# Merging the weight loads and pairing two K tiles at the start of a decode kernel, with V moved to the low regions of the buffer

## The chip, the cores and the metric

One core of a Trainium2 chip (trn2). The metric is the device time of one execution in microseconds (us). The runs of the kernel before lie within about 0.1% of each other. A profile is one execution; its span is shorter than the timed execution (before: 381.4 against 383.2). A run would be set aside as slow if it took over 1.5% more than the fastest of the same kernel. The engines' names: PE multiplies matrices, PEld loads its weights, DVE is the vector engine, ACT (ScalarE) the scalar one, POOL is GpSimd, and SP here only issues loads.

## The reference, cut to what matters

One decode step. Attention with 32 query heads over 4 K/V heads of 65,536 positions by 128 (here: S = 65536, four heads of K and V, 134 MB in bfloat16), and beside it a gated MLP on the same row x. Sizes of the weights: wq 1024x4096, w_in 1024x3584, w_out 1792x1024, wo 4096x1024.

```python
q = (x @ wq)                                  # 32 heads of 128
scores = einsum('bhqd,bhkd->bhqk', q, k) * Dh ** -0.5
a = einsum('bhqk,bhkd->bhqd', softmax(scores), v) ... @ wo
z = gelu(x @ w_in); z1, z2 = halves of z      # z2 goes through a layernorm
b = (z1 * (w_sp * layernorm(z2) + b_sp)) @ w_out
g = sigmoid((x * gate_w).sum())
return g * a + (1 - g) * b
```

Everything is read once: 162.01 MB.

## The kernel before

All large inputs go through one SBUF buffer `kv` of five regions (0 to 4), 32 KB in each of 128 partitions. A K or V tile of one head (one of four) fills one region. All large loads are issued by one engine's queue (SP), in program order, and each waits until the instructions that last used its region are done. The 16 DMA engines then take the loads in that order.

```python
NKV = 5                                        # regions
def load(src, shape, at): ...                  # one DMA into region `at`
def load_kv(src, g, j, at, n=1): ...           # n tiles of head g from tile j on, one DMA

win_t = [load(win_view[:, i * KH:(i + 1) * KH, :], (KH, F), 3 + i) for i in range(2)]
wq_t = [load(wq_view[:, i * KH:(i + 1) * KH, :], (KH, HD), 1 - i) for i in range(2)]
...
def k_tile(g, j, kn):                          # scores of one K tile
    for v in range(VC):                        # four quarters
        nc.vector.transpose(...)               # DVE, 2.3 us
        while late:
            nc.vector.reduce_max(**late.pop()) # row maximum of the tile before
        ...                                    # 8 matmuls
    nc.scalar.copy(out=sct[g, j][:], in_=s_ps[:])
def stats(g): ...                              # maximum, exponentials, transposes of p
def v_tile(g, j, vt): ...                      # 32 matmuls
...
build_w(0)
for j in range(NT):                            # head 0
    k_tile(0, j, load_kv(A_k_cache, 0, j, (2, 1, 0, 3)[j])[0])
    if j == 1:
        build_w(1)
project(load(B_w_out..., (FC, D), 4), FC, uT, 0, first=True)
stats(0)
for g in range(1, G):
    for h in range(2):
        kn = load_kv(A_k_cache, g, 2 * h, 1 - h, 2)
        for i in ((0, 1), (1, 0))[h]:
            k_tile(g, 2 * h + i, kn[i])
        if h == 0 and g + 1 < G:
            build_w(g + 1)
        vn = load_kv(A_v_cache, g - 1, 2 * h, 3, 2)
        v_tile(g - 1, 2 * h, vn[0])
        if h == 1:
            stats(g)
        v_tile(g - 1, 2 * h + 1, vn[1])
    head_out(g - 1)
for j, n, at in ((0, 2, 1), (2, 1, 3), (3, 1, 4)):
    ...                                        # last V tiles, then wo in pieces, then the output
```

In what follows K1.23 means tiles 2 and 3 of K's head 1, loaded as one pair.

Of the kernel before, what the change touches and what calls it, by code (L numbers as in the profile page):

```python
# [22 lines left out]
ZN = 448  # L23
HN = 512
WO_SPLIT = ((16,), (8, 4, 2, 1, 1))
# [3 lines left out]
def kernel(  # L29
# [17 lines left out]
    _, _, D = A_x.shape  # L47
    _, G, S, DH = A_k_cache.shape
    HD = A_wq.shape[1]
    H = HD // DH  # L50
    REP = H // G
    F = B_w_in.shape[1]
    FH = F // 2
    KC = D // P
    FC = FH // P
    OC = HD // P
    QD = P // H
    NT = S // (P * CT)
# [20 lines left out]
    def same_weights(ins):  # L79
        held.add(ins.ins.name)  # L80
# [79 lines left out]
    def load(src, shape, at):  # L160
        n = 1
        for s in shape:
            n *= s
        v = kv[:, int(at * CT * P):int(at * CT * P) + n]
        if len(shape) == 2:
            v = v.rearrange("p (a b) -> p a b", b=shape[1])
        ins = nc.sync.dma_start(out=v, in_=src)  # L167
        if not first_load:
            first_load.append(ins.ins.name)
        return v  # L170

    def load_kv(src, g, j, at, n=1):
        h, i = divmod(j, 2)
        rows = src[0, g, 2 * h * CT * P:2 * (h + 1) * CT * P, :].rearrange(
            "(p c) d -> p (c d)", c=2 * CT)
        v = load(rows[:, i * CT * DH:(i + n) * CT * DH], (n * CT * DH,), at)
        return [v[:, i * CT * DH:(i + 1) * CT * DH] for i in range(n)]
# [8 lines left out]

    KH = KC // 2
    win_view = B_w_in.rearrange("(p c) n -> p c n", c=KC)
    win_t = [load(win_view[:, i * KH:(i + 1) * KH, :], (KH, F), 3 + i) for i in range(2)]
    wq_view = A_wq.rearrange("(p c) n -> p c n", c=KC)  # L190
    wq_t = [load(wq_view[:, i * KH:(i + 1) * KH, :], (KH, HD), 1 - i) for i in range(2)]


    row = const.tile([P, P], FP32, name="row")
# [25 lines left out]
    def one_hot(shape, dtype, in0, col, name):  # L220
# [13 lines left out]
                     start=True, stop=True)  # L234
# [37 lines left out]
    def x_rows(ps, w, n, i):  # L272
        for c in range(KH):
            for t in range(NB):
                for k in range(F // (NB * ZN) if n == ZN else NHB):
                    o = (k * NB + t) * n
                    ins = nc.tensor.matmul(  # L277
                        ps[t * B:(t + 1) * B, k * HN:k * HN + n],
                        lhsT=xT[:, i * KH + c:i * KH + c + 1].to_broadcast([P, B]),
                        rhs=w[:, c, o:o + n], start=(i == 0 and c == 0),  # L280
                        stop=(i == 1 and c == KH - 1), skip_group_check=True)
                    if k > 0:
                        same_weights(ins)

    z_ps = pss.tile([P, 2 * HN], FP32, name="z_ps", tag="s")
    for i in range(2):
        x_rows(z_ps, win_t[i], ZN, i)
    rowt = big.tile([P, 2 * HN], FP32, name="rowt")
    om8 = rowt[:].rearrange("p (x d) -> p x d", d=DH)
    zm = rowt[:, :2 * ZN].rearrange("p (h j c) -> p h j c", h=2, c=FC)  # L290
# [41 lines left out]
    uT = const.tile([P, FC], BF16, name="uT")  # L332
# [3 lines left out]

    q_ps = pss.tile([P, 2 * HN], FP32, name="q_ps", tag="s")
    for i in range(2):
        x_rows(q_ps, wq_t[i], HN, i)
    NX = NHB * HH * 2  # L340
    qm = rowt[:].rearrange("p (x j e) -> p x j e", x=NX, e=2)
    for k in range(NHB):
# [3 lines left out]
                                                                   j=B, e=2),  # L346
# [11 lines left out]
                     rhs=q4[:].rearrange("p t x -> p (t x)"), start=True, stop=True)  # L358
# [8 lines left out]
    def build_w(g):  # L367
        for v in range(VC):
            nc.vector.tensor_tensor(
                out=wt[g % 2][:, v, :, :, v, :],  # L370
                in0=qs[:, g].unsqueeze(2).to_broadcast([P, BP, NB, REP]),
                in1=own_n[:].unsqueeze(1).unsqueeze(3).to_broadcast([P, BP, NB, REP]),
                op=ALU.mult)
# [5 lines left out]
    def k_tile(g, j, kn):  # L379
        kb = kn.bitcast(I32)  # L380
        n = CC * DH // 2
        s_ps = pss.tile([P, 2 * HN], FP32, name="s_ps", tag="s")
        for v in range(VC):
            nc.vector.transpose(out=kb[:, v * n:(v + 1) * n], in_=kb[:, v * n:(v + 1) * n])  # L384
            while late:
                nc.vector.reduce_max(**late.pop())  # L386
            kx = kn[:, v * CC * DH:(v + 1) * CC * DH].rearrange(
                "p (c h k e) -> p h e c k", h=2, k=B, e=2)
            for b in range(BP):
                for k in range(2):  # L390
                    ins = nc.tensor.matmul(  # L391
                        s_ps[:, k * HN:(k + 1) * HN],
                        lhsT=wt[g % 2][:, v, b].rearrange("p a v h -> p (a v h)"),
                        rhs=kx[:, b // 2, b % 2, k * CC // 2:(k + 1) * CC // 2, :],
                        start=(v == 0 and b == 0), stop=(v == VC - 1 and b == BP - 1),
                        skip_group_check=True)
                    if k > 0:
                        same_weights(ins)
        if g not in mxs:
            mxs[g] = wk.tile([P, NT], FP32, name="mx")  # L400
        sct[g, j] = scp.tile([P, CC * B], BF16, name="sc")
        nc.scalar.copy(out=sct[g, j][:], in_=s_ps[:])  # L402
        late.append(dict(out=mxs[g][:, j:j + 1], in_=sct[g, j][:], axis=AX.X))
# [26 lines left out]
    def v_tile(g, j, vt):  # L430
        if j == 0:
            o_ps[g] = pso.tile([P, 2, VC * DH], FP32, name="o_ps")
        vx = vt.rearrange("p (v c d) -> p c v d", v=VC, d=DH)
        for u in range(CC // 2):
            hs = slice(u % 2 * P // 2, (u % 2 + 1) * P // 2)
            for e in range(2):
                ins = nc.tensor.matmul(  # L437
                    o_ps[g][hs, e, :],
                    lhsT=ptt[g, j][:, 2 * u:2 * u + 2, :].rearrange("p c x -> p (c x)"),
                    rhs=vx[:, 2 * u + e], start=(j == 0 and u < 2),  # L440
                    stop=(j == NT - 1 and u >= CC // 2 - 2), skip_group_check=True)
                if e > 0:
                    same_weights(ins)
# [31 lines left out]
    def project(w, n, vec, c0, first=False, last=False):  # L475
        for c in range(n):
            for t in range(NB):
                nc.tensor.matmul(  # L478
                    out_ps[t * B:(t + 1) * B, :],
                    lhsT=vec[:, c0 + c:c0 + c + 1].to_broadcast([P, B]),  # L480
                    rhs=w[:, c, t * NO:(t + 1) * NO],
                    start=(first and c == 0), stop=(last and c == n - 1),
                    skip_group_check=True)


    build_w(0)
    for j in range(NT):
        k_tile(0, j, load_kv(A_k_cache, 0, j, (2, 1, 0, 3)[j])[0])
        if j == 1:
            build_w(1)  # L490
    project(load(B_w_out.rearrange("(p c) n -> p c n", c=FC), (FC, D), 4), FC, uT, 0, first=True)
    stats(0)
    for g in range(1, G):
        for h in range(2):
            kn = load_kv(A_k_cache, g, 2 * h, 1 - h, 2)
            for i in ((0, 1), (1, 0))[h]:
                k_tile(g, 2 * h + i, kn[i])
            if h == 0 and g + 1 < G:
                build_w(g + 1)
            vn = load_kv(A_v_cache, g - 1, 2 * h, 3, 2)  # L500
            v_tile(g - 1, 2 * h, vn[0])
            if h == 1:
                stats(g)
            v_tile(g - 1, 2 * h + 1, vn[1])
        head_out(g - 1)
    for j, n, at in ((0, 2, 1), (2, 1, 3), (3, 1, 4)):
        for i, vt in enumerate(load_kv(A_v_cache, G - 1, j, at, n)):
            v_tile(G - 1, j + i, vt)
    head_out(G - 1)
# [1 line left out]

    wo_view = A_wo.rearrange("(p c) n -> p c n", c=OC)
    c0 = 0
    for at, split in enumerate(WO_SPLIT):
        for n in split:
            t = load(wo_view[:, c0:c0 + n, :], (n, D), at + c0 % (OC // 2) * D / (CT * P))
            project(t, n, oa, c0, last=(c0 + n == OC))
            c0 += n
# [46 lines left out]
```

## Time and profile before

| kernel before | |
|---|---|
| time | 383.24 us (median of 3), 383.21 (5, later) |
| span of the profile | 381.4 us |
| DMA, read from HBM | 162.01 MB, 425 GB/s over the span |
| busy: PE / DVE / ACT | 61% / 57% / 10% |

The page of the kernel before: busy tenths of the DMA engines in 40 slices of the span, what they moved in each, and the sum.

```profile
DMA  9999999999999999999999999999999999999995
GB/s 376 439 426 416 433 436 440 436 461 429 400 426 440 440 435 426 440 440 440 440 428 440 440 440 433 428 427 406 433 440 428 426 433 427 440 411 436 440 405 230
HBM read 162.01 MB, written 0.00 MB: 425 GB/s over the span
```

The DMA row is full up to the last slice. Throughput in three stretches (start:end, length, busy time of PE, PEld, DVE, ACT and POOL, PE's clock, mean busy share of the DMA engines, GB/s):

```profile
core 0: us, PE busy (x) PEld busy (x) DVE busy (x) ACT busy (x) POOL busy (x), PEclk, DMA share, GB/s
40.00:90.00 50.00, 32.56 (x140) 6.28 (x65) 42.28 (x35) 3.04 (x3) 0.00 (x0) 0.84 1.00 430
90.00:170.00 80.00, 50.23 (x273) 11.67 (x167) 47.97 (x33) 10.29 (x14) 0.00 (x0) 0.80 1.00 433
170.00:370.00 200.00, 130.26 (x727) 30.22 (x373) 114.94 (x96) 22.71 (x33) 0.00 (x0) 0.83 1.00 431
```

430 to 433 GB/s throughout. The Trainium skill ("DMA: Bandwidth & Descriptors", Specifications) gives 435 GB/s as the ceiling of the fabric, and the trace agrees. So the kernel is bound by DMA, and what matters is whether the DMA queue ever runs empty. That is read from when SP issues a load. The timeline of SP (start us, duration, what):

```profile
71.85 0.33 SPq L167 DMA_DIRECT2D kv<-in_A_k_cache_dram  x1
95.97 0.33 SPq L167 DMA_DIRECT2D kv<-in_A_v_cache_dram  x1
119.21 0.33 SPq L167 DMA_DIRECT2D kv<-in_A_k_cache_dram  x1
137.86 0.33 SPq L167 DMA_DIRECT2D kv<-in_A_v_cache_dram  x1
```

These four are K1.01, V0.01, K1.23 and V0.23. The packet records of the trace say when the engines came to them: the mean of the 16 engines had finished the load ahead of V0.01 at 105.3, of K1.23 at 124.7 and of V0.23 at 144.1 us. So each was issued 5.5 to 9 us before it was needed. Call that the lead: the mean time at which the engines finish all that was issued earlier, less the time of the issue.

DVE after head 0's first K tile (the number in brackets is idle time, and what ended it):

```profile
59.84 2.31 DVE L384 STREAM_TRANSPOSE kv<-kv 128x2048 int32<-128x2048 int32 x1 [2.12 <-DMA kv<-in_A_k_cache_dram]
62.07 1.20 DVE L386 TENSOR_REDUCE mx<-sc 128x1 f32<-128x1024 bf16 x1
63.18 6.69 DVE L384 STREAM_TRANSPOSE kv<-kv 128x2048 int32<-128x2048 int32 x3
```

DVE waits 2.1 us for tile 1, which lands while PE still works on tile 0.

### The profile page before, as it was taken

What the parts mean: (1) busy time and instruction counts of PE and PEld (TensorE: products, weight loads), DVE (VectorE), ACT (ScalarE), POOL (GpSimd) and SP (SyncE); (2) the same over time, 40 slices, a digit from 0 to 9 for tenths busy, and PEclk for the clock granted to TensorE, in tenths of its full rate; (3) what the DMA queues carried; (4) which work ended last, traced back from release to release, by engine and by line L of the source; (5) the groups of instructions that cost most, each with busy time, mean ns of one, the idle gap of its engine ahead of it and who ended that gap; (6) DMA issues with size and microseconds to landing.
All of it is one profiled execution on the core that took longest, in us unless ns stands there. A gap on an engine that the chain in (4) does not pass through costs nothing.

```text
span 381.4 us, 2581 instructions
## 1 busy us (share of the span) xinstructions
PE 232.4 (61%) x1372; PEld 56.8 (15%) x796; DVE 218.4 (57%) x211; ACT 39.6 (10%) x55; POOL 4.4 (1%) x10
## 2 busy tenths in 40 slices
PE   0433467678157944796397629872967196849355
PEld 0110011112011210121011101120111011212123
DVE  4241487996687506966977059669780488550040
ACT  1010001111601100114010001050001010500000
POOL 4000000000000000000000000000000000000000
PEclk9966659998759895989588959895799679969766
DMA  9999999999999999999999999999999999999995
GB/s 376 439 426 416 433 436 440 436 461 429 400 426 440 440 435 426 440 440 440 440 428 440 440 440 433 428 427 406 433 440 428 426 433 427 440 411 436 440 405 230
DMA packets 4375, 162.17 MB, mean 425 GB/s; under 512 B 520, under 2 KB 524, under 8 KB 908
## 3 DMA queue, kind: packets, MB, share of 16 engines
q1 hardware_dynamic: 4324, 162.01, 98.7%
q8 instruction: 8, 0.13, 0.1%
q14 instruction: 3, 0.02, 0.0%
q10 hardware_dynamic: 40, 0.01, 0.0%
HBM read 162.01 MB, written 0.00 MB: 425 GB/s over the span
## 4 chain that ended last, share of the span: by engine, by line
DMA 59%; PE 20%; DVE 16%; issue 2%; ACT 1%; SPq 1%; DVEq 0%; ACTq 0%
DMA kv<-in_A_k_cache_dram 37%; PE s_ps L391 15%; DVE kv L384 9%; DMA kv<-in_A_wo_dram 8%; DMA kv<-in_A_wq_dram 7%; DMA kv<-in_A_v_cache_dram 7%; PE o_ps L437 3%; DVE pt L427 2%; DVE mx L386 1%; DVE o_sb L451 1%; PE q_ps L277 1%; ACT sc L424 1%; DVE rowt L447 1%; ACT sc L402 1%; SPq L167 1%
## 5 line engine op out<-in xcount | busy, mean ns | idle before, releaser
L391 PE MATMUL s_ps<-kv,wt 128*128 128x512 bf16 x512 | 142.1, 437 | 81.8 <-DVE kv L384 81.7
L384 DVE STREAM_TRANSPOSE kv<-kv 128x2048 int32<-128x2048 int32 x64 | 142.7, 2280 | 55.5 <-DMA kv<-in_A_k_cache_dram 55.5
L437 PE MATMUL o_ps<-kv,pt 128*64 128x512 bf16 x512 | 61.6, 399 | 7.7 <-DMA kv<-in_A_v_cache_dram 7.7
L391 PEld LDWEIGHTS <-wt 128*128 128x128 bf16 x256 | 27.5, 108 | 197.6 <-issue 140.2
L402 ACT CAST sc<-s_ps 128x1024 bf16<-128x1024 f32 x16 | 16.2, 1013 | 253.5 <-PE s_ps L391 253.5
L437 PEld LDWEIGHTS <-pt 128*64 128x64 bf16 x256 | 16.0, 115 | 50.7 <-issue 48.1
L427 DVE STREAM_TRANSPOSE pt<-sc 128x1024 bf16<-128x1024 bf16 x16 | 18.6, 1217 | 6.8 <-ACT sc L424 6.8
L386 DVE TENSOR_REDUCE mx<-sc 128x1 f32<-128x1024 bf16 x12 | 14.5, 1207 | 10.1 <-ACT sc L402 10.1
L424 ACT ACTIVATE sc<-sc,nb 128x1024 bf16<-128x1024 bf16 x16 | 18.2, 1137 | 12.2 <-DVE nb L420 12.2
L447 DVE TENSOR_TENSOR rowt<-o_ps,own 128x1024 f32<-128x1024 f32 x4 | 4.8, 1194 | 24.9 <-PE o_ps L437 24.9
L457 PE MATMUL om_ps<-o_sb,hsel 128*32 128x128 f32 x8 | 2.5, 421 | 19.7 <-DVE o_sb L451 19.7
L406 DVE TENSOR_REDUCE mx<-sc 128x1 f32<-128x1024 bf16 x4 | 4.9, 1220 | 14.2 <-ACT sc L402 14.2
L277 PE MATMUL q_ps<-kv,xT 128*32 128x512 bf16 x64 | 7.2, 627 | 7.4 <-DMA kv<-in_A_wq_dram 7.4
L478 PE MATMUL out_ps<-kv,oa 128*32 128x256 bf16 x128 | 6.7, 366 | 3.7 <-DMA kv<-in_A_wo_dram 2.2
L277 PE MATMUL z_ps<-kv,xT 128*32 128x448 bf16 x64 | 6.2, 570 | 3.8 <-DMA kv<-in_B_w_in_dram 3.8
L344 DVE TENSOR_TENSOR rowt<-q_ps,own_b 128x512 f32<-128x512 f32 x2 | 1.3, 686 | 12.5 <-PE q_ps L277 12.5
L451 DVE TENSOR_REDUCE o_sb<-rowt 128x128 f32<-128x1024 f32 x4 | 7.5, 1872 | 0.1
L292 DVE TENSOR_TENSOR rowt<-z_ps,own_b 128x448 f32<-128x448 f32 x2 | 1.2, 620 | 8.5 <-PE z_ps L277 8.5
L233 PE MATMUL xb_ps<-xg,spread 8*128 8x256 bf16 x1 | 0.4, 367 | 9.1 <-DMA xg<-in_gate_w_dram 9.1
L277 PEld LDWEIGHTS <-xT 128*32 128x32 bf16 x64 | 3.0, 139 | 19.4 <-issue 19.3
L478 PEld LDWEIGHTS <-oa 128*32 128x32 bf16 x128 | 4.4, 124 | 6.1 <-issue 3.3
L521 ACT CAST out_sb<-out_ps 128x256 bf16<-128x256 f32 x1 | 0.4, 372 | 45.4 <-PE out_ps L478 45.4
(88 smaller groups left out, 54.8 us busy)
## 6 DMA issues: line engine op xcount, KB each, us to landing
kv<-in_A_k_cache_dram SPq DMA_DIRECT2D x4, 4096.0 KB, 26.8
kv<-in_A_wq_dram SPq DMA_DIRECT2D x2, 4096.0 KB, 32.8
kv<-in_A_v_cache_dram SPq DMA_DIRECT2D x2, 4096.0 KB
kv<-in_B_w_in_dram SPq DMA_DIRECT2D x2, 3584.0 KB, 15.0
kv<-in_A_wo_dram SPq DMA_DIRECT2D x1, 4096.0 KB
kv<-in_B_w_out_dram SPq DMA_DIRECT2D x1, 3584.0 KB
kv<-in_A_wo_dram SPq DMA_DIRECT2D x1, 2048.0 KB, 28.6
kv<-in_A_wo_dram SPq DMA_DIRECT2D x1, 1024.0 KB, 30.7
```

Of the source, the lines that this page charges most:

```text
L277: ins = nc.tensor.matmul(ps[t * B:(t + 1) * B, k * HN:k * HN + n], lhsT=xT[:, i * KH + c:i * KH + c + 1].to_broadcast([P, B]), rhs=w[:, c, ...
L384: nc.vector.transpose(out=kb[:, v * n:(v + 1) * n], in_=kb[:, v * n:(v + 1) * n])
L386: nc.vector.reduce_max(**late.pop())
L391: ins = nc.tensor.matmul(s_ps[:, k * HN:(k + 1) * HN], lhsT=wt[g % 2][:, v, b].rearrange("p a v h -> p (a v h)"), rhs=kx[:, b // 2, b % 2, ...
L402: nc.scalar.copy(out=sct[g, j][:], in_=s_ps[:])
L406: nc.vector.reduce_max(**late.pop())
L424: nc.scalar.activation(out=sct[g, j][:], in_=sct[g, j][:], func=ACT.Exp, scale=SCALE, bias=nb[:, 0:1], accum_out=lss[g][:, j:j + 1])
L427: nc.vector.transpose(out=ptt[g, j][:].rearrange("p c x -> p (c x)"), in_=sct[g, j][:])
L437: ins = nc.tensor.matmul(o_ps[g][hs, e, :], lhsT=ptt[g, j][:, 2 * u:2 * u + 2, :].rearrange("p c x -> p (c x)"), rhs=vx[:, 2 * u + e], sta ...
L447: nc.vector.tensor_tensor(out=om8, in0=o_ps[g][:].rearrange("p e (v d) -> p (e v) d", d=DH), in1=own_8[:].unsqueeze(2).to_broadcast([P, 2 ...
L451: nc.vector.tensor_reduce(out=o_sb[:], in_=om8.rearrange("p x d -> p d x"), axis=AX.X, op=ALU.add)
L478: nc.tensor.matmul(out_ps[t * B:(t + 1) * B, :], lhsT=vec[:, c0 + c:c0 + c + 1].to_broadcast([P, B]), rhs=w[:, c, t * NO:(t + 1) * NO], st ...
```

## The change

Its intent is fewer and larger loads: w_in as one load of 56 KB a partition and wq as one of 64 KB (each was two halves); in head 0, K tiles 0 and 1 as a pair behind tile 2, so that the stream is tile 2, pair 0 and 1, tile 3. To make room, the regions are mirrored: V goes to regions 0 and 1, K's pairs to 2 to 4.

```diff
-    win_t = [load(win_view[:, i * KH:(i + 1) * KH, :], (KH, F), 3 + i) for i in range(2)]
+    win_t = load(win_view, (KC, F), 3)
-    wq_t = [load(wq_view[:, i * KH:(i + 1) * KH, :], (KH, HD), 1 - i) for i in range(2)]
+    wq_t = load(wq_view, (KC, HD), 0)
 ... (the matmuls on them take w[:, i * KH + c, ...]) ...
-    for j in range(NT):
-        k_tile(0, j, load_kv(A_k_cache, 0, j, (2, 1, 0, 3)[j])[0])
-        if j == 1:
+    for j, n, at in ((2, 1, 2), (0, 2, 3), (3, 1, 1)):
+        for i, kn in enumerate(load_kv(A_k_cache, 0, j, at, n)):
+            k_tile(0, j + i, kn)
+        if j == 2:
             build_w(1)
-    project(load(B_w_out..., (FC, D), 4), FC, uT, 0, first=True)
+    project(load(B_w_out..., (FC, D), 0), FC, uT, 0, first=True)
     stats(0)
     for g in range(1, G):
         for h in range(2):
-            kn = load_kv(A_k_cache, g, 2 * h, 1 - h, 2)
-            for i in ((0, 1), (1, 0))[h]:
+            kn = load_kv(A_k_cache, g, 2 * h, 2 + h, 2)
+            for i in ((1, 0), (0, 1))[h]:
 ...
-            vn = load_kv(A_v_cache, g - 1, 2 * h, 3, 2)
+            vn = load_kv(A_v_cache, g - 1, 2 * h, 0, 2)
 ... (the last V tiles and wo are mirrored alike) ...
```

More of the change, by code (lines that the diff above doesn't have):

```diff
@@ L279, in x_rows @@
                         lhsT=xT[:, i * KH + c:i * KH + c + 1].to_broadcast([P, B]),
-                        rhs=w[:, c, o:o + n], start=(i == 0 and c == 0),
+                        rhs=w[:, i * KH + c, o:o + n], start=(i == 0 and c == 0),
                         stop=(i == 1 and c == KH - 1), skip_group_check=True)
@@ L286 @@
     for i in range(2):
-        x_rows(z_ps, win_t[i], ZN, i)
+        x_rows(z_ps, win_t, ZN, i)
     rowt = big.tile([P, 2 * HN], FP32, name="rowt")
@@ L338 @@
     for i in range(2):
-        x_rows(q_ps, wq_t[i], HN, i)
+        x_rows(q_ps, wq_t, HN, i)
     NX = NHB * HH * 2
@@ L486 @@
     build_w(0)
-    for j in range(NT):
-        k_tile(0, j, load_kv(A_k_cache, 0, j, (2, 1, 0, 3)[j])[0])
-        if j == 1:
+    for j, n, at in ((2, 1, 2), (0, 2, 3), (3, 1, 1)):
+        for i, kn in enumerate(load_kv(A_k_cache, 0, j, at, n)):
+            k_tile(0, j + i, kn)
+        if j == 2:
             build_w(1)
-    project(load(B_w_out.rearrange("(p c) n -> p c n", c=FC), (FC, D), 4), FC, uT, 0, first=True)
+    project(load(B_w_out.rearrange("(p c) n -> p c n", c=FC), (FC, D), 0), FC, uT, 0, first=True)
     stats(0)
@@ L505 @@
         head_out(g - 1)
-    for j, n, at in ((0, 2, 1), (2, 1, 3), (3, 1, 4)):
+    for j, n, at in ((0, 2, 2), (2, 1, 1), (3, 1, 0)):
         for i, vt in enumerate(load_kv(A_v_cache, G - 1, j, at, n)):
@@ L513 @@
     c0 = 0
-    for at, split in enumerate(WO_SPLIT):
+    for at, split in zip((4, 2), WO_SPLIT):
         for n in split:
```

## The prediction

> **What bounds the kernel now.** The DMA engines. The page's DMA row is 9 in all 40 slices but the last, with 162.01 MB read at 425 GB/s over 381.4 us. In the trace's packet records the 16 engines are busy 376.3 us each between the first packet (1.0 us) and the last (378.4): about 1.1 us idle. A 65,536-byte packet takes 2.423 us; 16 engines of that are 433 GB/s. The Trainium skill ("DMA: Bandwidth & Descriptors", Specifications) gives 435 GB/s as the fabric ceiling, and the trace agrees. PE is 61% busy, DVE 57%. The change can only open or close holes in the DMA stream.
>
> **What it removes.** No bytes. Three loads fewer, each with one 4-byte packet per engine of about 8 ns. Packets double in size: 32,768 bytes take 1.213 us, 65,536 take 2.423, so 3 ns saved a packet, 24 packets an engine. Sum: about -0.1 us.
>
> **What it moves (estimates from trace durations).** The DMA stream keeps its times, but computing starts later:
> - w_in: the z matmuls (6.2 us) start at 19.7 us in one piece; off the path (q isn't needed before 39).
> - wq: lands at 39.1 as before, but then 64 matmuls (7.1 us) follow instead of 32 (3.6). The first K tile ends at about 62.5 (61.0 before).
> - The pair lands as one at about 68.9; before, its first half started at 59.8. PE and DVE sit idle. A tile from standing takes 12.2 us, following ones 10.8 to 11.6 (cast, row maximum, three transposes, the last quarter of matmuls). So the last tile of head 0 ends at about 103 instead of 94.3, and w_out's 56 matmuls at about 105 instead of 95.9.
>
> Slack before: V's first pair was issued at 95.97, the engines came to it at 104.3 to 106.7; head 1's second K pair was issued at 119.2, needed at 123.6 to 126.1; V's second pair at 137.9, needed at 143.0 to 145.6.
>
> After: V's first pair issues at about 105; the first load took 1.0 us from issue to first packet. Early engines wait up to 2 us, the last none: no loss. Head 0's statistics end at about 114.7 (105.65 before), so DVE starts on head 1's K tile there instead of at 107.2, and frees region 3 at about 126.7. The second K pair's first packets come at about 127.7, where the last engine runs dry at about 126.4: a hole of 1 to 1.5 us on the slowest engine, 2 to 3 on others. V's second pair issues at about 145.4, needed at 147: barely no hole. From then on waits are tied to landings again, with 3.5 us of slack or more (regions are only mirrored), and the delay stays at about 1.2 us. The tail is the same.
>
> **Predicted time:** 383.24 - 0.1 + 1.2 = 384.4 us; 8 in 10: 382.5 to 387.0. Faster by over 2%: 0.01; within 2%: 0.96; slower by over 2%: 0.03.
>
> **What would show it.** Transposes idle from about 62 to 69 us, waiting for K's pair; q matmuls in one block from 39.1; V's first pair issued at 104 to 106, head 1's second K pair at 126 to 128, after the engines ran dry; idle of an engine up from 1.1 us to 2 to 5; dips of throughput near 105 and 127 us; head 3's issues about 1.2 us later.
>
> **What would make it wrong.** If tiles after the idle stretch run at 10.8 us each (PE unthrottled) the hole closes and the time is 383.2. If PE is throttled more, or the next issue also comes late (margin under 1 us), two holes add up to 3 us or more. If larger first packets ramp differently, it moves by tenths.

## The result

| | before | after |
|---|---|---|
| time, median of 5 | 383.21 us (383.12 to 383.49) | 387.19 us (386.68 to 388.12) |
| span of the profile | 381.4 us | 385.3 us |
| HBM read | 162.01 MB, 425 GB/s | 162.01 MB, 420 GB/s |

The ratio is 1.0105, 95% interval 1.0091 to 1.0119: slower by 1%, within 2%. (A ratio here is the mean time of one kernel's fast runs over that of the other's of the same rounds, so not quite the ratio of the medians.) The time lies 0.2 us above the range of the prediction, and the loss, 4.0 us, is over three times the 1.2 that was predicted.

The page of the kernel after, the same rows:

```profile
DMA  9998998999799999999999999999999999999994
GB/s 381 490 435 378 485 433 388 423 448 435 335 429 435 415 430 395 429 422 429 429 437 435 435 435 435 430 436 435 435 435 430 435 435 429 435 406 432 432 412 192
HBM read 162.01 MB, written 0.00 MB: 420 GB/s over the span
```

There are now slices at 7 and 8 tenths; single slices of GB/s are noisy, because a packet of 64 KB lasts a quarter of a slice. The three stretches are steadier:

```profile
40.00:90.00 50.00, 30.02 (x149) 6.00 (x70) 33.21 (x30) 2.02 (x2) 0.00 (x0) 0.75 1.00 432
90.00:170.00 80.00, 51.21 (x286) 11.82 (x172) 56.88 (x38) 10.98 (x14) 0.00 (x0) 0.87 0.98 417
170.00:370.00 200.00, 130.59 (x735) 30.55 (x378) 111.19 (x91) 23.02 (x33) 0.00 (x0) 0.85 1.00 431
```

Before 90 us and after 170 us the stream is as fast as it was. Between them it moved 417 GB/s instead of 433: (1 - 417/433) x 80 us = 3.0 us of lost transfer. So most of the 4 us come from this stretch, and from nothing that lasts. SP's issues there:

```profile
81.71 0.33 SPq L167 DMA_DIRECT2D kv<-in_A_k_cache_dram  x1
105.07 0.33 SPq L167 DMA_DIRECT2D kv<-in_A_v_cache_dram  x1
125.51 0.33 SPq L167 DMA_DIRECT2D kv<-in_A_k_cache_dram  x1
144.14 0.33 SPq L167 DMA_DIRECT2D kv<-in_A_v_cache_dram  x1
```

V0.01, K1.23 and V0.23 are issued 9.1, 6.3 and 6.3 us later than before. Why they are late is in DVE's timeline and in the chain of waits (start us, duration, what):

```profile
59.09 0.86 DVE L369 TENSOR_TENSOR wt<-qs,own_n 128x128 bf16<-128x128 bf16 x4
69.71 2.31 DVE L384 STREAM_TRANSPOSE kv<-kv 128x2048 int32<-128x2048 int32 x1 [9.77 <-DMA kv<-in_A_k_cache_dram]
```

```profile
25.46 44.16 DMA kv<-in_A_k_cache_dram
69.71 2.31 DVE kv L384
...
101.49 1.91 PE s_ps L391 x8
...
110.11 4.64 DVE pt L427 x4
114.75 2.21 DVE kv L384
117.05 8.44 PE s_ps L391 x32
125.51 23.27 DMA kv<-in_A_k_cache_dram
```

DVE idles 9.8 us for the pair. From its landing at 69.6 us to the issue at 125.5 us the chain runs over DVE, ACT and PE without a wait for a DMA: three K tiles, head 0's statistics, head 1's first K tile. Whatever delays its start delays the issues at its end, and these come when the DMA queue is empty or nearly so. The packet records around the issue of V0.01 (worked out from the trace, whose records name no engine; "dry" is when an engine finished its part of the load before):

```
V0.01 issued 105.07
 engines dry             104.51 to 105.49 (15 engines), 106.87 (the last)
 their next packets      106.02 to 106.59 (15 engines), 108.11 (the last)
 that packet took        2.7 to 3.4 us   (a packet of 65,536 bytes in a full queue: 2.42)
```

Fifteen engines stand still for 1 to 2 us, and their first packet is slow too. The last engine, which was still busy when the load was issued, starts 1.2 us after it ran dry all the same, and its first packet takes 3.42 us.

### The profile page after: what moved, and what is told of

Read it like the earlier page. It is cut to its first block, busy times and chain, and to the rows that moved or that the text cites. A ratio compares the mean times of both kernels' runs of the same rounds, so it can differ in the third digit from the quotient of the medians.

```text
span 385.3 us, 2576 instructions
## 1 busy us (share of the span) xinstructions
PE 227.0 (59%) x1372; PEld 56.2 (15%) x796; DVE 218.2 (57%) x211; ACT 39.6 (10%) x55; POOL 4.4 (1%) x10
## 3 DMA queue, kind: packets, MB, share of 16 engines
q1 hardware_dynamic: 3892, 162.01, 98.0%
HBM read 162.01 MB, written 0.00 MB: 420 GB/s over the span
## 4 chain that ended last, share of the span: by engine, by line
DMA 58%; DVE 21%; PE 15%; issue 3%; ACT 2%; SPq 0%; ACTq 0%; DVEq 0%
DMA kv<-in_A_k_cache_dram 39%; DVE kv L384 14%; PE s_ps L391 11%; DMA kv<-in_A_wo_dram 8%; DMA kv<-in_A_v_cache_dram 7%; DMA wb<-in_B_b_sp_dram 4%; PE o_ps L437 2%; DVE pt L427 2%; DVE mx L386 2%; PE z_ps L277 1%; ACT sc L402 1%; ACT sc L424 1%; DVE o_sb L451 0%; SPq L167 0%; ACT L424 0%
## 5 line engine op out<-in xcount | busy, mean ns | idle before, releaser
L391 PE MATMUL s_ps<-kv,wt 128*128 128x512 bf16 x512 | 137.7, 424 | 87.2 <-DVE kv L384 86.9
L437 PE MATMUL o_ps<-kv,pt 128*64 128x512 bf16 x512 | 62.6, 404 | 7.5 <-DMA kv<-in_A_v_cache_dram 7.5
L277 PE MATMUL q_ps<-kv,xT 128*32 128x512 bf16 x64 | 6.4, 589 | 8.2 <-DMA kv<-in_A_wq_dram 8.2
L277 PE MATMUL z_ps<-kv,xT 128*32 128x448 bf16 x64 | 5.1, 501 | 0.0
```

The costliest lines, as they stand in the source:

```text
L277: ins = nc.tensor.matmul(ps[t * B:(t + 1) * B, k * HN:k * HN + n], lhsT=xT[:, i * KH + c:i * KH + c + 1].to_broadcast([P, B]), rhs=w[:, i ...
L391: ins = nc.tensor.matmul(s_ps[:, k * HN:(k + 1) * HN], lhsT=wt[g % 2][:, v, b].rearrange("p a v h -> p (a v h)"), rhs=kx[:, b // 2, b % 2, ...
L437: ins = nc.tensor.matmul(o_ps[g][hs, e, :], lhsT=ptt[g, j][:, 2 * u:2 * u + 2, :].rearrange("p c x -> p (c x)"), rhs=vx[:, 2 * u + e], sta ...
```

## The experiments

Theory A: the pair makes computing start 9 us late, loads are issued when the DMA engines have run dry, and a late issue costs more than I reckoned. Theory B: the merged w_in and wq, which make q later, are what pushes. Theory C: the new regions or the larger packets slow the stream themselves. Eight kernels ran, in two groups with one chip each; all gave correct results. The kernel before ran beside each group, at 383.22 (11 runs) and 383.21 us (9 runs).

### e1_k_single: the pair undone, the rest kept

```diff
-    for j, n, at in ((2, 1, 2), (0, 2, 3), (3, 1, 1)):
+    for j, n, at in ((0, 1, 2), (1, 1, 3), (2, 1, 4), (3, 1, 1)):
-        if j == 2:
+        if j == 1:
```

> The kernel after, with head 0's four K tiles loaded one by one in the order 0,1,2,3 (merged w_in and wq and the mirrored regions stay). Theory A (the pair makes the computing of head 0 end 9 us late, so V's first pair and head 1's second K pair are issued when the DMA engines have run dry): the first transposes after tile 0 start by about 60 us, w_out's matmuls end at about 97, V's first pair is issued at about 96 to 98, no hole, time 382.8 to 383.5. Theory B (the merged w_in and wq, which make q 3 us late, are what pushes): V's first pair still issued after 102, time 386 or more. Theory C (the new regions or the 64 KB packets themselves slow the stream, whatever the issue times): time 386 or more with early issues.

Measured: 383.21 us (383.01 to 383.31), ratio to the kernel before 0.9998 (0.9985 to 1.0011). SP's issues of V0.01, K1.23 and V0.23, and the stretch from 90 to 170 us:

```profile
96.51 0.33 SPq L167 DMA_DIRECT2D kv<-in_A_v_cache_dram  x1
119.09 0.33 SPq L167 DMA_DIRECT2D kv<-in_A_k_cache_dram  x1
136.98 0.33 SPq L167 DMA_DIRECT2D kv<-in_A_v_cache_dram  x1
```

```profile
90.00:170.00 80.00, 49.51 (x276) 11.53 (x167) 49.26 (x34) 10.36 (x14) 0.00 (x0) 0.83 1.01 435
```

The issues are back where they were, the stretch is at full rate, and the whole 4 us are gone, though w_in and wq are merged, V lies in the low regions, and 64 KB packets carry all the rest. B and C fall. It also shows what the merged weights and the new regions are worth by themselves: nothing that the time shows.

### e2_weights_split: the pair kept, w_in and wq in halves again

```diff
-    win_t = load(win_view, (KC, F), 3)
+    win_t = [load(win_view[:, i * KH:(i + 1) * KH, :], (KH, F), 3 + i) for i in range(2)]
-    wq_t = load(wq_view, (KC, HD), 0)
+    wq_t = [load(wq_view[:, i * KH:(i + 1) * KH, :], (KH, HD), 1 - i) for i in range(2)]
```

> The kernel after, with w_in and wq loaded in halves again as before (only the K pair and the regions are left of the change). Theory A: the pair lands at about 69.7 as in the kernel after, V's first pair is issued at 104.5 to 105.5, time 386.5 to 388. Theory B: time back at 383.2 to 384. Theory C: 385 to 387.5, with fewer slow packets.

Measured: 387.58 us (386.70 to 388.26), ratio 1.0113 (1.0100 to 1.0126). V0.01 was issued at 106.0 us, a little later than I expected, and the stretch from 90 to 170 us moved 417 GB/s as in the kernel after:

```profile
106.03 0.33 SPq L167 DMA_DIRECT2D kv<-in_A_v_cache_dram  x1
90.00:170.00 80.00, 52.57 (x285) 12.11 (x172) 55.21 (x38) 10.98 (x14) 0.00 (x0) 0.83 0.98 417
```

So the pair carries the loss without the merged weights. The new regions stay in this run; e1_k_single has shown that they cost nothing without the pair.

### e3_pair_last: the pair at the end of head 0

```diff
-    for j, n, at in ((2, 1, 2), (0, 2, 3), (3, 1, 1)):
+    for j, n, at in ((0, 1, 2), (1, 1, 3), (2, 2, 0)):
-        if j == 2:
+        if j == 1:
-    project(load(B_w_out..., (FC, D), 0), FC, uT, 0, first=True)
+    project(load(B_w_out..., (FC, D), 4), FC, uT, 0, first=True)
```

> The kernel after, with tiles 0 and 1 of head 0 singly and tiles 2 and 3 as the pair (in wq's regions; w_out in region 4). Theory A: DVE waits for the pair only from about 73 to 78 us, so head 0 ends at about 101 instead of 103.4; V's first pair, which now waits for the last tile alone, is issued at about 101, 3.5 us before it is needed, without loss; head 1's second K pair is issued at about 123 with 0.5 to 1 us of lead, which costs about 1 us. Time 383.6 to 384.8, between the two kernels. Theories B and C: 386.5 or more.

Measured: 385.52 us (384.53 to 385.99), ratio 1.0057 (1.0045 to 1.0068): between the two kernels, but 0.7 us over the range I gave. V0.01 was issued at 102.3 instead of 101, K1.23 at 124.4 instead of 123: I had let the pair land with the mean engine, but DVE waits for the last one, which finished its part of the pair at 78.9 us where the mean finished at 77.0. The 90 to 170 us stretch moved 426 GB/s, between 433 and 417.

### e4_delay5: a late issue alone, first attempt

Five dummy copies on ScalarE, written to region 3 of the kernel before, ahead of the load of V1.01 (issued at 178.1 us before), so that this load has to wait for them.

```diff
+            if (g, h) == (2, 0):
+                for _ in range(5):
+                    nc.scalar.copy(out=kv[:, 3 * CT * P:3 * CT * P + 1024],
+                                   in_=kv[:, 3 * CT * P:3 * CT * P + 1024])
             vn = load_kv(A_v_cache, g - 1, 2 * h, 3, 2)
```

> The kernel before, with five dummy ScalarE copies on region 3 ahead of V's load of tiles 0 and 1 for head 1 (issued at 178.1, needed at 182.3 to 184.3), so that it is issued at about 184.4, once, with nothing else moved. It measures what one late issue costs. Theory A with a price for the restart (about 1 us from issue to the first packet and 0.6 to 0.8 us more in every engine's first packet): mean end of the engines 3.0 to 3.5 us later, the latest engine 2 to 3 us, time 385.2 to 386.5. My prediction's price (only the dry time, the latest engine loses nothing or little): 383.3 to 384.5.

Measured: 417.33 us (417.12 to 418.44). The design was wrong. ScalarE works in program order, and the copies stood behind its casts of head 2's scores, so they ran at 210 us and not at 179:

```profile
210.35 5.35 ACT L502 COPY kv<-kv 128x1024 bf16<-128x1024 bf16 x5
215.73 0.33 SPq L167 DMA_DIRECT2D kv<-in_A_v_cache_dram  x1
```

It still measures the price of an issue into an empty queue, with a very large dose. The mean engine ran dry at 182.89 us, the load was issued at 215.73, and the mean engine finished it at 236.89. In a full queue the load takes 19.39 us (8 packets of 2.423 us and the small one). So 236.89 - 215.73 - 19.39 = 1.77 us went by beyond the wait for the issue.

### e5_delay2 and e5_delay5: a late issue alone, mended

The same copies, two or five, placed right behind head 1's exponentials, where ScalarE is free.

```diff
             v_tile(g - 1, 2 * h + 1, vn[1])
+            if (g, h) == (1, 1):
+                for _ in range(5):          # 2 in the other
+                    nc.scalar.copy(out=kv[:, 3 * CT * P:3 * CT * P + 1024],
+                                   in_=kv[:, 3 * CT * P:3 * CT * P + 1024])
         head_out(g - 1)
```

> The kernel before, with two dummy ScalarE copies on region 3 right after head 1's exponentials, so that V's load that was issued at 178.1 us is issued at about 181.6, 1.3 us before the engines run dry at 182.9 (mean). One late issue, nothing else moved. Theory A with a fixed lead (a load must be issued about 1.8 us, up to 3, before the engines run dry; what is missing of that is lost on all engines): mean end of that load 0.6 to 1.1 us later, time 383.6 to 384.6. My prediction's price (no loss as long as the issue comes 1 us before the queue is empty): 383.1 to 383.4.

> The same with five copies: issued at about 184.8, 1.9 us after the mean engine is dry. Theory A with a fixed lead of 1.8: mean end 3.5 to 4.0 us later, time 386.2 to 387.2. My prediction's price (issue plus 1.0 us for the first packet, nothing for slow first packets, the latest engine hardly hit): the latest engine runs dry at 184.3, so it would lose 1.5: 384.7.

Measured: two copies 384.65 us (383.87 to 384.74), ratio 1.0032 (1.0018 to 1.0046); five copies 386.81 us (386.65 to 387.19), ratio 1.0096 (1.0082 to 1.0110). ScalarE and SP with five copies:

```profile
179.29 5.33 ACT L507 COPY kv<-kv 128x1024 bf16<-128x1024 bf16 x5
184.65 0.33 SPq L167 DMA_DIRECT2D kv<-in_A_v_cache_dram  x1
```

One load, issued 6.6 us later than before in an otherwise unchanged kernel, costs 3.6 us, nearly as much as the whole change. With two copies it was issued at 180.6, a microsecond earlier than I had reckoned and 2.2 us ahead of the mean engine's need, and still cost 0.7 us on that load. The time, 1.4 us more, is just above the range I gave, and the price that the expectation ascribes to my prediction (no loss with 1 us of lead) is refuted.

### e6_wout_first: the first hole made smaller

```diff
     for j, n, at in ((2, 1, 2), (0, 2, 3), (3, 1, 1)):
+        if j == 3:
+            project(load(B_w_out..., (FC, D), 0), FC, uT, 0, first=True)
         for i, kn in enumerate(load_kv(A_k_cache, 0, j, at, n)):
 ...
-    project(load(B_w_out..., (FC, D), 0), FC, uT, 0, first=True)
```

> The kernel after, with w_out loaded and multiplied ahead of head 0's last K tile instead of behind it, so that V's first pair waits for that tile alone: issued at about 103.4 instead of 105.07. Head 1's second K pair is issued at 125.5 as before. If the latest late issue decides (a stream that has lost little at the first hole runs dry earlier at the second): the first hole costs 0.5 to 1.0 us instead of 2.2, the second 2.2 to 2.6 instead of 1.1, and the time stays at 386.5 to 387.4. If each hole adds its own cost: 385.4 to 386.2.

Measured: 386.91 us (386.11 to 387.81), ratio 1.0098 (1.0084 to 1.0111), so in effect the time of the kernel after. V0.01 was issued at 103.7 us and its hole shrank to 0.65 us. But K1.23's grew to 3.54 us.

```profile
103.66 0.33 SPq L167 DMA_DIRECT2D kv<-in_A_v_cache_dram  x1
126.78 0.33 SPq L167 DMA_DIRECT2D kv<-in_A_k_cache_dram  x1
```

Part of that comes with this run: K1.23's issue moved from 125.5 to 126.8 us. Head 1's first tile started 0.2 us later, and 12 of its 32 matmuls started about 0.43 us apart before the pace went to 0.22, instead of 7 in the kernel after. Whether my edit caused that was not tested. In both kernels K1.23 ends about 2 us plus its 19.4 us after its issue (148.05 after 126.78; 146.93 after 125.51), whatever was lost at the hole before. So what the first hole no longer costs, the second does. How much the time would have gained with the issue left at 125.5 us, this run does not show; by that sum, very little.

### e7_free_regions: computing late, issues early

The pair stays where the change put it. In head 1, V's first four tiles and K's tiles 2 and 3 are loaded singly into regions that are free earlier; the regions of the later heads are mirrored to suit.

```diff
-            kn = load_kv(A_k_cache, g, 2 * h, 2 + h, 2)
+            if (g, h) == (1, 1):
+                kn = [load_kv(A_k_cache, 1, 2 + i, (0, 3)[i])[0] for i in range(2)]
+            else:
+                kn = load_kv(A_k_cache, g, 2 * h, 2 if g == 1 else h, 2)
 ...
-            vn = load_kv(A_v_cache, g - 1, 2 * h, 0, 2)
+            if g == 1:
+                vn = [load_kv(A_v_cache, 0, 2 * h + i, ((4, 1), (2, 4))[h][i])[0]
+                      for i in range(2)]
+            else:
+                vn = load_kv(A_v_cache, g - 1, 2 * h, 3, 2)
 ... (the last V tiles and wo likewise) ...
```

> The kernel after, with head 0 still loaded with the late pair, but head 1's second K pair and V's first two pairs loaded as single tiles into regions that are free early (issued at about 92.6, 103.4, 105.1, 125.5, 137, 140.6 us, each 6 us or more before it is needed, the first 10). Computing is as late as in the kernel after (head 0's last tile ends at 103.4, head 1's first tile at about 125.5). Theory A (late issues cost the time, not late computing): no hole, time 382.9 to 383.7. If late computing or the pair by itself costs the time: 386 or more.

Measured: 383.35 us (383.23 to 383.49), ratio 1.0005 (0.9992 to 1.0017). SP's issues of V0.0 and V0.1 (one line, from the first to the end of the second), then of K1.2 and K1.3, and the 90 to 170 us stretch:

```profile
91.93 11.18 SPq L167 DMA_DIRECT2D kv<-in_A_v_cache_dram  x2
104.44 22.14 SPq L167 DMA_DIRECT2D kv<-in_A_k_cache_dram  x2
```

```profile
90.00:170.00 80.00, 58.35 (x350) 14.15 (x207) 59.11 (x43) 14.11 (x18) 0.00 (x0) 0.89 1.01 433
```

V0.0 is issued at 91.9 and K1.2 at 104.4 us, and the stretch is back at 433 GB/s. Head 0 is computed as late as in the kernel after: K1.3, which waits for head 1's first tile, is issued at about 126.3 us. So it is not late computing that costs the time, but what late computing does to the issues.

### The price of a late issue, from all runs

For each late load: lead (mean dry time less issue) and loss (mean end of the load, less mean dry time, less its time in a full queue), from the packet records.

| run, load | lead us | loss us | lead + loss |
|---|---|---|---|
| e4_delay5, V1.01 | -32.84 | 34.61 | 1.77 |
| e5_delay5, V1.01 | -1.80 | 3.67 | 1.87 |
| e6_wout_first, K1.23 | -1.67 | 3.54 | 1.87 |
| e2_weights_split, V0.01 | -0.93 | 2.72 | 1.79 |
| after, V0.01 | -0.22 | 2.16 | 1.94 |
| e3_pair_last, K1.23 | 0.43 | 1.63 | 2.06 |
| e2_weights_split, K1.23 | 0.71 | 1.33 | 2.04 |
| after, K1.23 | 0.90 | 1.13 | 2.03 |
| e6_wout_first, V0.01 | 1.41 | 0.65 | 2.06 |
| e5_delay2, V1.01 | 2.23 | 0.72 | |
| V0.23 of e6_wout_first, e2_weights_split, e3_pair_last, after; V0.01 of e3_pair_last | 2.6 to 2.8 | 0.02 to 0.49 | |
| before, e1_k_single, all pairs of K and V | over 4 | 0.12 at most | |

Up to a lead of 1.4 us the loss is 1.8 to 2.1 us less the lead. From 2.2 to 2.8 us it scatters between nothing and 0.7, and beyond 4 us it is gone. About two thirds of the price is the time from the issue to an engine's first packet (in e4_delay5 0.95 us for the first engine, 1.25 for the mean one), the rest is that this packet is slow (there 2.99 us on average instead of 2.42). The very first packets of the kernels show the same surcharge whatever their size: 1.68 instead of 1.06 us for 28 KB packets before, 2.75 instead of 2.12 us for 56 KB packets after, 0.6 us each.

The Trainium skill ("DMA: Bandwidth & Descriptors", Anatomy of one DMA) puts a fixed cost of about 2.0 us on each DMA, measured for DMAs issued from GpSimd, and puts most of it after the last byte, in the wait for the confirmation that it has landed. The size is near the 1.8 to 2.1 us of these SP loads, but that need not be the same cost: here the time goes before and in the first packet. After the last packet little is left: in the kernel after, the pair's last packet ends at 69.12 us and the wait for it at 69.62. The page's "Rules for kernel authors" say that an early issue overlaps the fixed cost; the loads with over 4 us of lead agree, with a loss of 0.12 us at most.

## Why the prediction was right or wrong, point by point

- "What bounds the kernel now. The DMA engines": right. e1_k_single and e7_free_regions have very different computing and the same time within 0.1%.
- "Sum: about -0.1 us" for fewer, larger packets: small, as predicted, if not that small. Until w_out's end, ahead of any hole, the mean engine is 0.4 us earlier after than before (85.49 against 85.86), and 0.2 in e1_k_single; none of it shows in a time.
- The timing of the compute side: right within 1.3 us. w_out's matmuls were to end "at about 105" (105.02), V's first pair to be issued "at about 105" (105.07), the statistics to end "at about 114.7" (114.75), region 3 to be free "at about 126.7" (125.51), V's second pair to be issued "at about 145.4" (144.14). The one difference is a tile, head 1's first, of 10.8 us where I had taken about 12: its matmuls start 0.43 us apart and later 0.22 us, and the pace changed after 7 of 32, in the kernel before after 13. The two paces are what the Trainium skill states for a cold and a warm array ("TensorE: Matmul & The Clock Gate", "Wait — 56ns, not 53.3ns?") for 512 columns. Such a tile stands in the prediction as one that would make it wrong by closing the hole; it came, and the hole stayed.
- The step that failed: "Early engines wait up to 2 us, the last none: no loss", and with it the price that I set for K1.23, first packets 1.0 us after the issue and no slow packet. V0.01 in fact cost the mean engine 2.16 us. Its last engine, still busy at the issue, lost 1.2 us before its first packet and 1.0 us in it. Then K1.23 cost 1.13 us and V0.23, which I had as "barely no hole" and which came with 2.8 us of lead, 0.30. Together 3.6 us; less the 0.5 us that the mean engine was ahead by the end of K1.01, that is about the 3.0 us by which it ends later (377.47 before, 380.48 after).
- The mis-sized term: the price of an issue into an empty queue. I took 1.0 us; it is 1.8 to 2.1 us, and it is due in part up to 2.8 us of lead. With 1.9 us in its place, my own issue times give V0.01 a loss of 1.6 (lead 0.3) and K1.23 one of 2.3 (the engines then run dry at 126.3), 3.9 together, and 383.24 - 0.1 + 3.9 = 387.0 us. Measured: 387.19. (That sum is made after the fact.)
- "The delay stays" and "The tail is the same": right for the mean engine. After 170 us the stream moves 431 GB/s in both kernels.
- What stays open: the time rose by 4.0 us, the mean engine's end by 3.0. The rest is the spread of the engines: the latest is 2.1 us behind the mean at the end of wo's third piece in the profile of after, 1.0 in that of before. That spread differs from profile to profile (1.3 in e2_weights_split, 2.0 in e3_pair_last), as do the times of the kernels with a hole (1.4 us between the fastest and slowest run of after, 0.4 before). The traces show where the last microsecond arises, not why it falls there: besides the loads each trace has eight packets of 16 KB of the kind "instruction", each on one engine for about 1 us, and the data packet behind it takes 2.9 instead of 2.4 us. In after one of them ran at 249.97 us on an engine that was behind already, and over that load the latest engine's lag on the mean grew from 1.1 to 2.3 us; in e3_pair_last the one at 195.40 us did the same. In before only the first ones did, and of the 1.5 us of lag that they made 1.0 is left at the end.

No version beat the kernel before: e1_k_single ties with it (0.9998), e7_free_regions too (1.0005).

## What to carry to other kernels

When DMA is the bound and its queue is full, see first what larger loads can gain (here nothing); what they change is when data lands, when computing starts and so when buffers come free for later loads. List for each load the time between its issue and the moment at which the engines reach it, before and after a change, and keep at least 3 to 4 us of it (nothing was measured here between 2.8 and 3.6 us); with under about 1.5 us, count about 2 us, minus the lead, for the mean engine. An engine that is still busy at the issue can lose as much. Of several late issues in a row, mending an earlier one alone gained nothing that the time shows (386.91 against 387.19 us, with the later issue 1.3 us later than it was), and free buffers mended all of them without making the computing any earlier (383.35 us).

## What the Trainium skill lacked or had wrong

- "DMA: Bandwidth & Descriptors" (Latency and other measured facts) gives 0.6 us to the first byte for loads issued from SP. Here 0.95 to 1.0 us pass from the start of the issue to the first packet of the first engine, about 0.62 from the end of SP's 0.33 us issue, so the figure holds if it is counted from there, which the page does not say; the mean engine's first packet comes about 1.2 us after the start of the issue into an empty queue. What the page lacks is the whole price of finding the queue empty, 1.8 to 2.1 us: its fixed cost of about 2.0 us was measured for DMAs issued from GpSimd and is put mostly after the last byte, where only about 0.5 us pass here.
- No page says how early a load must be issued for the stream to stay full. Here 2.2 us still cost 0.7 us in one run and 2.6 to 2.8 us up to 0.5; over 4 us cost 0.12 us at most.
- No page says that the first packet on an engine after a hole is slower by much the same amount whatever its size: 0.6 to 0.7 us on average, for packets of 28, 56 and 64 KB (the first two at the start of the kernels).
- The rule of the same page to batch loads to 1 MiB or more has no upper end and says nothing of when the data can be used: here loads of 4 MB and 8 MB stream alike (1.213 us for a packet of 32 KB, 2.423 for one of 64 KB), and the larger one delayed by over 9 us what needs only its first half.
